# A decode block on one core: w_down's rows and the gate/up columns dealt anew over the partitions, part of them loaded by GpSimd

## The chip, the cores and the metric

One core of one Trainium2 chip. The metric is the device time of one launch in microseconds, the median of the runs shown; lower is better. The kernel before takes 1370.03 us (median of 3 runs, 1370.01 to 1370.21).

## The reference

One token of a decode step. Two branches read the same layer-normed row and are added to the input: attention with a cached K and V of 16384 positions in 32 heads, and a gated feed-forward layer.

```python
D, H, Sk, Dh, Df = 576, 32, 16384, 128, 4608

def _A_ref(x, k_cache, v_cache, wq, wo):
    q = (x @ wq).reshape(B, Sq, H, Dh).transpose(0, 2, 1, 3)
    scores = jnp.einsum("bhqd,bhkd->bhqk", q, k_cache) * (Dh ** -0.5)
    p = _softmax(scores, axis=-1)
    o = jnp.einsum("bhqk,bhkd->bhqd", p, v_cache)
    return o.transpose(0, 2, 1, 3).reshape(B, Sq, H * Dh) @ wo

def _B_ref(x, w_gate, w_up, w_down):
    h = _gelu(x @ w_gate) * (x @ w_up)
    return h @ w_down

xn = _layernorm(x)
return x + _A_ref(xn, ...) + _B_ref(xn, ...)
```

Everything is float32. K and V together are 32 x 2 x 8.4 MB; the weights are wq and wo with 9.4 MB each and w_gate, w_up and w_down with 10.6 MB each.

## The kernel before, in words

All large loads go through SP's queue (`load`, L69, the line under which the profile shows them), in the order in which the code writes them: wq, gate and up, then K and V head by head, then w_down and wo. Four places in SBUF take turns: two K buffers (`kslot`), one V buffer (`vslot`), and small tiles. Each load waits until the earlier user of its buffer is done.

**Projections (`project`, L139).** A weight matrix of 576 rows lies with four rows on each of 128 partitions; the last 64 rows (the tail) are split in two halves of columns so that they also fill 128 partitions. The output columns are dealt to four quarters; quarter q is written to output partitions 32q to 32q+31, so four matmuls use four column groups of TensorE. `sizes` says into which three blocks of one PSUM bank each a quarter's columns are cut. For gate and up a quarter has 4608 / 4 = 1152 columns (`FG`), in blocks of 396, 396 and 360.

**Gate and up (`ffn`).** Column f of gate and up must end on the partition that holds row f of w_down. w_down is loaded with 36 consecutive rows on each partition (`WD_T`), so partition p needs columns 36p to 36p+35. After the matmuls each of the 32 partitions of a quarter holds the whole quarter's row. VectorE multiplies it by the mask `same` (L176), which keeps the partition's own columns, and sums over the 32 groups (L179), which leaves `gu`, 128 x 36 for gate and for up. `ffn_act` makes the activation `hT`, 128 x 36, from it.

**Heads.** For each head VectorE multiplies K by q (L215) and sums (L216), a softmax follows, and TensorE multiplies V by the probabilities (L236, `pv`). K tile h+1 and V tile h are loaded meanwhile.

**The end.** With the last V tile on its way, SP issues w_down in two pieces (`WD_PIECES`: 28 rows a partition into the V buffer `ta`, 8 into the K buffer `tb`) and wo in six (`WO_PIECES`: 16 rows into `tb`, then 8, 4, 2, 1 and 1 into the last buffer `te`). `ta` comes free when TensorE has read the V tile of head 30, `tb` when VectorE has used the K tile of head 31, `te` when TensorE has read the V tile of head 31. TensorE then adds row by row into the output (`add_out`, L281): two matmuls of 288 columns a row, or four of 144 for the last 8 rows of wo. VectorE copies the sum, and ACT stores it as four rows.

GpSimd issues no transfer. Its only work is at the start (a memset and the identity matrix). ACT's queue carries three one-row loads of x and the output.

Of the kernel before, what the change touches and what calls it, by code (L numbers as in the profile page):

```python
# [8 lines left out]
F32 = mybir.dt.float32  # L9
AF = mybir.ActivationFunctionType  # L10
ALU = mybir.AluOpType
AX = mybir.AxisListType

P = 128
H, SK, DH = 32, 16384, 128
D, DF = 576, 4608
# [3 lines left out]
DM = P * DJ  # L20
# [3 lines left out]
HD = H * DH  # L24
QG, QB = HD // 4, 512
QS = HD // 2
WD_T = DF // P
FG = DF // 4
FB = (11 * WD_T, 11 * WD_T, 10 * WD_T)
WO_T = HD // P  # L30
WD_PIECES = (28, 8)
WO_PIECES = (16, 8, 4, 2, 1, 1)
WO_A = 16
WO_Q = 8
QUART = D // 4
HG = 4
# [5 lines left out]
def kernel(ctx: ExitStack, tc: tile.TileContext, x, k_cache, v_cache, wq, wo, wg, wu, wd, out):  # L42
    nc = tc.nc
    cpool = ctx.enter_context(tc.tile_pool(name="cpool", bufs=1))
# [12 lines left out]
    wmain = {n: w[:DM].rearrange("(p j) f -> p (j f)", j=DJ) for n, w in (("q", wq), ("g", wg), ("u", wu))}  # L57
    wtail = {n: w[DM:].rearrange("d (s f) -> (d s) f", s=2) for n, w in (("q", wq), ("g", wg), ("u", wu))}
    wov = wo.rearrange("(p t) f -> p (t f)", t=WO_T)
    wdv = wd.rearrange("(p t) f -> p (t f)", t=WD_T)  # L60

    def kslot():
        return kpool.tile([P, R * DH], F32, tag="k", name="kslot")

    def vslot():
        return vpool.tile([P, R * DH], F32, tag="v", name="vslot")

    def load(dst, src):
        nc.sync.dma_start(dst, src)  # L69
        return dst  # L70

    ROW3 = 3 * DF
    wq_t, wg_t, mix = kslot(), kslot(), vslot()
    qt = load(wg_t[:, ROW3 : ROW3 + QS], wtail["q"])
    load(wq_t, wmain["q"])
    row3, tails, at = {}, {}, 0
# [2 lines left out]
        tails[n] = load(mix[:, at + DF : at + DF + DF // 2], wtail[n])  # L79
        at += DF + DF // 2  # L80

    xrow = mix[:1, ROW3 + FG : ROW3 + FG + D]
    nc.scalar.dma_start(xrow, xf)
    x2 = cpool.tile([P, HALF], F32, name="x2")
    nc.gpsimd.memset(x2, 0.0)
# [11 lines left out]
    same = cpool.tile([P, 32], F32, name="same")  # L97
# [15 lines left out]
    xm = xrow[:, :DM].rearrange("o (p j) -> o j p", j=DJ)  # L113
    for j in range(DJ):
        nc.tensor.matmul(px[:, j : j + 1], xm[:, j, :], ones[:1, :1], start=True, stop=True)
    xd = mix[:1, ROW3 + 2 * FG : ROW3 + 2 * FG + 2 * (D - DM)].rearrange("o (d s) -> o d s", s=2)
    nc.vector.tensor_copy(xd, xrow[:, DM:].unsqueeze(2).to_broadcast([1, D - DM, 2]))
    nc.tensor.matmul(px[:, DJ : DJ + 1], xd.rearrange("o d s -> o (d s)"), ones[:1, :1], start=True, stop=True)
    xp = cpool.tile([P, DJ + 1], F32, name="xp")
# [1 line left out]
    xnb = cpool.tile([P, DJ, 32], F32, name="xnb")  # L121
# [3 lines left out]
    xtb = cpool.tile([P, 2, 32], F32, name="xtb")  # L125
    nc.vector.tensor_copy(xtb, xt.unsqueeze(2).to_broadcast([P, 2, 32]))

    def project(steps, group, sizes):
        pg = ps_big.tile([P, 3, 512], F32, tag="pb", name="pg")
        for k, (j, rhs) in enumerate(steps):  # L130
            for b, size in enumerate(sizes):
                for q in range(4):
                    lo = q * group + sum(sizes[:b])
                    if j < DJ:
                        lhs = xnb[:, j, :]
                    else:
                        lhs = xtb[:, q // 2, :]
                        lo -= q // 2 * 2 * group
                    nc.tensor.matmul(pg[32 * q : 32 * q + 32, b, :size], lhs, rhs[:, lo : lo + size],  # L139
                                     start=k == 0, stop=k == len(steps) - 1)  # L140
        return pg

    steps = [(DJ, qt)] + [(j, wq_t[:, j * HD : (j + 1) * HD]) for j in range(DJ)]
    pq = project(steps, QG, (QB, QB))[:, :2, :]
    qrow = cpool.tile([P, QG], F32, name="qrow")
    nc.scalar.activation(qrow.rearrange("p (b f) -> p b f", f=QB), pq, AF.Copy)

# [2 lines left out]
    def q_spread(h):  # L150
        r = 32 * (h // (H // 4))
        lo = h % (H // 4) * DH
        pq = ps_s.tile([P, 512], F32, tag="sm", name="pq")
        nc.tensor.matmul(pq, ones[r : r + 1, :], qrow[r : r + 1, lo : lo + QH * DH], start=True, stop=True)  # L154
        return pq
# [4 lines left out]
        for i in range(QH):  # L160
            Q[h + i] = qs[:, i : i + 1, :]

    gu = cpool.tile([P, 2, WD_T], F32, name="gu")

    def ffn(which):
        n = "gu"[which]
        t = kslot() if which else wg_t
        steps = [(3, row3[n]), (DJ, tails[n])]
        load(t[:, :ROW3], wmain[n][:, :ROW3])
        steps += [(j, t[:, j * DF : (j + 1) * DF]) for j in range(DJ - 1)]  # L170
        pg = project(steps, FG, FB)
        gm = mix[:, ROW3 : ROW3 + FG].rearrange("p (m t) -> p m t", t=WD_T)
        at = 0
        for b, size in enumerate(FB):
            m = size // WD_T
            nc.vector.tensor_mul(gm[:, at : at + m, :], pg[:, b, :size].rearrange("p (m t) -> p m t", t=WD_T),  # L176
                                 same[:, at : at + m].unsqueeze(2).to_broadcast([P, m, WD_T]))
            at += m
        nc.vector.tensor_reduce(gu[:, which, :], gm.rearrange("p m t -> p t m"), axis=AX.X, op=ALU.add)  # L179

    ffn(0)
    ffn(1)

    hT = cpool.tile([P, WD_T], F32, name="hT")

    def ffn_act():
        g, u = gu[:, 0], gu[:, 1]
        t1 = cpool.tile([P, WD_T], F32, name="t1")
        tc.keep_in_program_order(nc.vector.tensor_mul(t1, g, g))
        tc.keep_in_program_order(nc.vector.tensor_scalar(t1, t1, 0.044715, 1.0, op0=ALU.mult, op1=ALU.add))  # L190
        tc.keep_in_program_order(nc.vector.tensor_mul(t1, t1, g))
        th = cpool.tile([P, WD_T], F32, name="th")
        nc.scalar.activation(th, t1, AF.Tanh, scale=0.7978845608028654)
        t2 = cpool.tile([P, WD_T], F32, name="t2")
        tc.keep_in_program_order(nc.vector.scalar_tensor_tensor(t2, th, 1.0, g, op0=ALU.add, op1=ALU.mult))
        tc.keep_in_program_order(nc.vector.scalar_tensor_tensor(hT, t2, 0.5, u, op0=ALU.mult, op1=ALU.mult))

# [51 lines left out]
    for h in range(H + 1):  # L249
        if h < H:  # L250
            KT[h], n = kslot(), R if h else SUB
            for i in range(0, R, n):
                load(KT[h][:, i * DH : (i + n) * DH], kv[h][:, i * DH : (i + n) * DH])
        if h > 0:
            VT[h - 1] = load(vslot() if h < H else kslot(), vv[h - 1])
        more = (h + 1) % QH == 0 and h + 1 < H
        pq = q_spread(h + 1) if more else None
        if h < H:
            for i in range(0, R, n):
                qk(h, i, n)  # L260
            KT.pop(h)
        if h == 0:
            ffn_act()
        if h > 0:
            pv(h - 1)
            if h % HG == 0:
                out_heads(h - HG)
        if more:
            q_take(h + 1, pq)
        if h < H:  # L270
            softmax(h)
# [6 lines left out]
    def add_out(groups, lhs, w, last=False):  # L278
        n = D // len(groups)
        for i, g in enumerate(groups):  # L280
            nc.tensor.matmul(g, lhs, w[:, i * n : (i + 1) * n], start=id(g) not in seen, stop=last)  # L281
            seen.add(id(g))

    half = [[pairs[i][32 * (2 * i + j) : 32 * (2 * i + j) + 1, :HALF] for j in range(2)] for i in range(2)]
    quart = [acc4[32 * g : 32 * g + 1, :] for g in range(4)]

    def load_rows(t, at, src, lo, n):
        load(t[:, at * D : (at + n) * D], src[:, lo * D : (lo + n) * D])
        return [t[:, (at + j) * D : (at + j + 1) * D] for j in range(n)]

    ta, tb, te = vslot(), kslot(), kslot()
    a, b = WD_PIECES
    wd_rows = load_rows(ta, 0, wdv, 0, a) + load_rows(tb, 0, wdv, a, b)
    wo_rows, lo = [], 0
    for n in WO_PIECES:
        wo_rows += load_rows(tb, b + lo, wov, lo, n) if lo < WO_A else load_rows(te, lo - WO_A, wov, lo, n)
        lo += n
# [13 lines left out]

    for j, w in enumerate(wd_rows):
        add_out(half[j % 2], hT[:, j : j + 1], w)

    for j, w in enumerate(wo_rows):
        if j < WO_T - WO_Q:
# [2 lines left out]
        if j == WO_T - 4:  # L319
            nc.vector.tensor_add(x2[:64], x2[:64], PO[0][64:, :HALF])  # L320
            nc.vector.tensor_add(x2[:64], x2[:64], acc[:64, :HALF])
            for i, g in enumerate(quart):
                r, lo = 32 * (i // 2), i % 2 * QUART
# [34 lines left out]
```

## Time and profile before

| what | value |
|---|---|
| median of 3 runs | 1370.03 us |
| the profiled execution | 1370.16 us |
| its span | 1368.3 us |
| bytes moved | 588.00 MB, mean 430 GB/s |
| VectorE busy | 1135.8 us (83%) |
| TensorE busy | 406.0 us (30%) |
| chain that ended last, by engine | DMA 51%, DVE 46%, PE 2% |

The span runs from the first to the last instruction; the time of the execution is 1.9 us longer. In the rows, a line such as L281 names the line of the kernel, `a<-b,c` the tile written and those read, `x56` a count. In the windows, DMA is the mean busy share of the 16 DMA engines in that stretch: 0.5 means that on average eight of them are at work. The chain is followed back from the last instruction, each piece with its start and its length.

### The profile page before, as it was taken

To read this page: it belongs to the slowest core of one execution; us is meant where nothing else is said; L and a number is where in the kernel's file an instruction comes from. 1 tells how busy PE (TensorE), PEld (TensorE's weight loads), DVE (VectorE), ACT (ScalarE), POOL (GpSimd) and SP (SyncE) were. 2 spreads that over 40 slices of the span, in tenths; PEclk is the share of its full clock that TensorE was granted. 3 is DMA by queue.
4 is the path that set the end of the run, shared out by engine and by line. 5 is a ranking of instruction groups with operands and counts; after the bars stand their busy time and mean duration, and the time that the engine had idled before them with its cause. 6 is when DMAs were issued, how large, how long until landed. Compare 5 with 4: busy or idle time off the path is not lost.

```text
span 1368.3 us, 6377 instructions
## 1 busy us (share of the span) xinstructions
PE 406.0 (30%) x2870; PEld 118.1 (9%) x2870; DVE 1135.8 (83%) x169; ACT 36.5 (3%) x126; POOL 1.0 (0%) x7
## 2 busy tenths in 40 slices
PE   4321233322311232323212332322213333221156
PEld 1110000100000000100000000100001000000012
DVE  1069999899888888898888888998888888988840
ACT  0000000000000000000000000000000000000000
POOL 0000000000000000000000000000000000000000
PEclk8775565565556556565566566565556555665577
DMA  9999999999999999999999999999999999999997
GB/s 404 440 425 450 430 429 430 430 435 432 437 435 429 431 430 439 432 432 435 431 436 433 433 431 430 435 432 439 435 430 430 431 432 437 438 435 428 429 428 336
DMA packets 11704, 588.00 MB, mean 430 GB/s; under 512 B 1303, under 2 KB 1309, under 8 KB 1694
## 3 DMA queue, kind: packets, MB, share of 16 engines
q1 hardware_dynamic: 11664, 587.60, 99.4%
q8 instruction: 22, 0.36, 0.1%
q14 instruction: 4, 0.03, 0.0%
q10 hardware_dynamic: 14, 0.01, 0.0%
HBM read 587.60 MB, written 0.00 MB: 429 GB/s over the span
## 4 chain that ended last, share of the span: by engine, by line
DMA 51%; DVE 46%; PE 2%; issue 0%; SPq 0%; ACT 0%; DVEq 0%
DMA kslot<-in_A_k_cache_dram 41%; DVE s L216 23%; DVE kslot L215 23%; DMA kslot<-in_A_v_cache_dram 3%; DMA kslot<-in_B_w_up_dram 3%; DMA kslot<-in_A_wo_dram 3%; DMA kslot<-in_A_wq_dram 2%; PE pg L139 1%; PE po L236 1%; DVE gu L179 0%; SPq L69 0%; PE pt L222 0%; DVE vslot L176 0%; DVE pm L220 0%; DVE nm L224 0%
## 5 line engine op out<-in xcount | busy, mean ns | idle before, releaser
L215 DVE TENSOR_TENSOR kslot<-kslot,qs 128x16384 f32<-128x16384 f32 (+1 forms) x33 | 551.3, 16705 | 88.4 <-DMA kslot<-in_A_k_cache_dram 86.9
L216 DVE TENSOR_REDUCE s<-kslot 128x128 f32<-128x16384 f32 (+1 forms) x33 | 551.2, 16703 | 3.3
L236 PE MATMUL po<-vslot,pe 128*16 128x512 f32 x1984 | 286.1, 741 | 645.0 <-DMA vslot<-in_A_v_cache_dram 645.0
L236 PEld LDWEIGHTS po<-vslot,pe 128*16 128x16 f32 x1984 | 67.3, 113 | 848.2 <-issue 848.2
L222 PE MATMUL pt<-ident,pm 128*1 128x128 f32 x32 | 11.9, 372 | 236.0 <-DVE pm L220 236.0
L176 DVE TENSOR_TENSOR vslot<-pg,same 128x396 f32<-128x396 f32 (+1 forms) x6 | 3.0, 552 | 69.1 <-PE pg L139 69.1
L139 PE MATMUL pg<-kslot,xnb 128*32 128x396 f32 (+2 forms) x208 | 23.6, 615 | 33.6 <-DMA kslot<-in_B_w_gate_dram 18.9
L228 ACT ACTIVATE nb<-pb 128x1 f32<-128x1 f32 x32 | 5.5, 171 | 812.4 <-PE pb L226 812.4
L320 DVE TENSOR_TENSOR x<-x,po 64x288 f32<-64x288 f32 x1 | 0.5, 457 | 30.8 <-PE po L281 30.8
L222 PEld LDWEIGHTS pt<-ident,pm 128*1 128x1 f32 x32 | 2.5, 79 | 259.4 <-DVE pm L220 218.5
L226 PE MATMUL pb<-nm,ones 1*128 1x1 f32 x64 | 18.1, 350 | 13.2 <-DVE nm L224 13.2
L224 DVE TENSOR_REDUCE nm<-pt 1x1 f32<-1x128 f32 x32 | 8.9, 278 | 14.9 <-PE pt L222 14.9
L226 PEld LDWEIGHTS pb<-nm,ones 1*128 1x128 f32 x64 | 15.8, 305 | 22.2 <-DVE nm L224 11.3
L154 PE MATMUL pq<-qrow,ones 1*128 1x512 f32 x16 | 15.6, 1073 | 0.0
L229 ACT ACTIVATE pe<-s,nb 128x128 f32<-128x128 f32 x32 | 12.8, 401 | 1.0
L302 DVE RECIPROCAL rl<-pl 128x32 f32<-128x32 f32 x1 | 0.4, 358 | 14.9 <-PE pl L300 14.9
L281 PE MATMUL acc<-kslot,oT 128*1 128x144 f32 (+1 forms) x112 | 10.5, 376 | 6.7 <-DMA kslot<-in_A_wo_dram 6.7
L139 PEld LDWEIGHTS pg<-kslot,xnb 128*32 128x32 f32 x208 | 7.1, 126 | 51.0 <-DMA kslot<-in_B_w_gate_dram 19.7
L241 ACT ACTIVATE o<-po 128x512 f32<-128x512 f32 x8 | 4.8, 597 | 222.0 <-PE po L236 222.0
L236 PE MATMUL po<-kslot,pe 128*16 128x512 f32 x64 | 9.6, 769 | 2.6 <-DMA kslot<-in_A_v_cache_dram 2.6
L281 PE MATMUL acc<-vslot,hT 128*1 128x288 f32 x56 | 8.6, 473 | 5.6 <-DMA vslot<-in_B_w_down_dram 5.6
L245 PE MATMUL pc<-same,o 128*128 128x4 f32 x64 | 8.4, 255 | 5.7 <-ACT o L241 5.7
(74 smaller groups left out, 109.9 us busy)
## 6 DMA issues: line engine op xcount, KB each, us to landing
kslot<-in_A_k_cache_dram SPq DMA_DIRECT2D x2, 4096.0 KB
vslot<-in_B_w_down_dram SPq DMA_DIRECT2D x1, 8064.0 KB
kslot<-in_B_w_gate_dram SPq DMA_DIRECT2D x1, 6912.0 KB, 54.0
kslot<-in_B_w_up_dram SPq DMA_DIRECT2D x1, 6912.0 KB
kslot<-in_A_wo_dram SPq DMA_DIRECT2D x1, 4608.0 KB, 39.2
vslot<-in_B_w_gate_dram SPq DMA_DIRECT2D x1, 2304.0 KB, 28.9
vslot<-in_B_w_up_dram SPq DMA_DIRECT2D x1, 2304.0 KB, 37.6
kslot<-in_B_w_down_dram SPq DMA_DIRECT2D x1, 2304.0 KB, 28.7
```

Source lines behind the costliest of these rows:

```text
L139: nc.tensor.matmul(pg[32 * q : 32 * q + 32, b, :size], lhs, rhs[:, lo : lo + size], start=k == 0, stop=k == len(steps) - 1)
L154: nc.tensor.matmul(pq, ones[r : r + 1, :], qrow[r : r + 1, lo : lo + QH * DH], start=True, stop=True)
L215: tc.keep_in_program_order(nc.vector.tensor_mul(blk, blk, Q[h].to_broadcast([P, n, DH])))
L216: nc.vector.tensor_reduce(S[h][:, i : i + n], blk, axis=AX.X, op=ALU.add)
L222: nc.tensor.transpose(pt[:1, :P], pm, ident)
L224: tc.keep_in_program_order(nc.vector.tensor_reduce(nm, pt[:1, :P], axis=AX.X, op=ALU.max, negate=True))
L226: nc.tensor.matmul(pb[:, :1], ones[:1, :], nm, start=True, stop=True)
L228: nc.scalar.activation(nb, pb[:, :1], AF.Copy, scale=SCALE)
L229: nc.scalar.activation(pe4, S.pop(h).rearrange("p (k s) -> p k s", s=4), AF.Exp, bias=nb, scale=SCALE, accum_out=lsum[:, h : h + 1])
L236: nc.tensor.matmul(PO[h // HG % 2][q : q + PW, :], pe[:, lo : lo + PW], vt[:, k * 512 : (k + 1) * 512], start=i == 0 and k < 4, stop=i == ...
L245: nc.tensor.matmul(pc[:, :HG], o4[:, j * DH : (j + 1) * DH], pick[:, j, :], start=j == 0, stop=j == 3)
L281: nc.tensor.matmul(g, lhs, w[:, i * n : (i + 1) * n], start=id(g) not in seen, stop=last)
```

## The change

w_down's rows are dealt unevenly. The first 128 x 33 = 4224 rows are loaded by SP with 33 rows on every partition (pieces of 16 and 17 for 28 and 8). The other 384 rows go to partitions 96 to 127, 12 on each, with four transfers from GpSimd's queue; transfer r takes partitions 96 + r, 100 + r, ..., 124 + r, eight rows of 12 x 2304 B. Before each of them goes a tiny GpSimd transfer of eight rows of 16 B into a part of the buffer that nobody reads.

The columns of gate and up follow: quarters of 32 x 33 = 1056 columns in blocks of 495, 495 and 66, and the last quarter has another 384 in its third block. Where a quarter's block crosses the middle of the tail's columns, its matmul is cut in two. A second, smaller product with the mask and a second sum fill columns 33 to 44 of `gu` on partitions 96 to 127; for the other partitions they stay zero. wo's first piece of 16 becomes 11 and 5, since `tb` now holds 17 rows of w_down. The row of x and a helper row move to another place of the same tile.

```diff
-WD_T = DF // P
-FG = DF // 4
-FB = (11 * WD_T, 11 * WD_T, 10 * WD_T)
+WD_T = 33
+WD_X = 12
+XP = 96
+DX = P * WD_T
+FT = WD_T + WD_X
+FG = 32 * WD_T
+FB = (15, 15, 2)
+FX = 32 * WD_X
 WO_T = HD // P
-WD_PIECES = (28, 8)
-WO_PIECES = (16, 8, 4, 2, 1, 1)
-WO_A = 16
+WD_PIECES = (16, 17)
+WO_PIECES = (11, 5, 8, 4, 2, 1, 1)
+WO_A = 11
...
-    wdv = wd.rearrange("(p t) f -> p (t f)", t=WD_T)
+    wdv = wd[:DX].rearrange("(p t) f -> p (t f)", t=WD_T)
+    wdx = wd[DX:].rearrange("(p t) f -> p (t f)", t=WD_X)
...
-    def project(steps, group, sizes):
+    def project(steps, total, bases, sizes):
         pg = ps_big.tile([P, 3, 512], F32, tag="pb", name="pg")
+        h = total // 2
         for k, (j, rhs) in enumerate(steps):
-            for b, size in enumerate(sizes):
+            for b in range(len(sizes[0])):
                 for q in range(4):
-                    lo = q * group + sum(sizes[:b])
+                    lo = bases[q] + sum(sizes[q][:b])
+                    hi = lo + sizes[q][b]
                     if j < DJ:
-                        lhs = xnb[:, j, :]
+                        parts = [(xnb[:, j, :], lo, hi, 0)]
                     else:
-                        lhs = xtb[:, q // 2, :]
-                        lo -= q // 2 * 2 * group
-                    nc.tensor.matmul(pg[32 * q : 32 * q + 32, b, :size], lhs, rhs[:, lo : lo + size],
-                                     start=k == 0, stop=k == len(steps) - 1)
+                        parts = [(xtb[:, i, :], max(lo, i * h), min(hi, i * h + h), i * h) for i in range(2)]
+                    for lhs, a, e, o in parts:
+                        if a < e:
+                            nc.tensor.matmul(pg[32 * q : 32 * q + 32, b, a - lo : e - lo], lhs, rhs[:, a - o : e - o],
+                                             start=k == 0, stop=k == len(steps) - 1)
...
-    gu = cpool.tile([P, 2, WD_T], F32, name="gu")
+    gu = cpool.tile([P, 2, FT], F32, name="gu")
+    nc.vector.memset(gu, 0.0)
+    fcols = [tuple(m * WD_T for m in FB)] * 3 + [tuple(m * WD_T + FX * (b == 2) for b, m in enumerate(FB))]
...
+        gx = mix[XP:, ROW3 + FG : ROW3 + FG + FX].rearrange("p (m t) -> p m t", t=WD_X)
+        nc.vector.tensor_mul(gx, pg[XP:, 2, FB[2] * WD_T : FB[2] * WD_T + FX].rearrange("p (m t) -> p m t", t=WD_X),
+                             same[XP:, :].unsqueeze(2).to_broadcast([32, 32, WD_X]))
+        nc.vector.tensor_reduce(gu[XP:, which, WD_T:], gx.rearrange("p m t -> p t m"), axis=AX.X, op=ALU.add)
...
-    wd_rows = load_rows(ta, 0, wdv, 0, a) + load_rows(tb, 0, wdv, a, b)
+    wd_rows = load_rows(ta, 0, wdv, 0, a)
+    junk = ta[0:32:4, (a + WD_X) * D : (a + WD_X) * D + 16]
+    for r in range(4):
+        tc.keep_in_program_order(nc.gpsimd.dma_start(junk[:, r * 4 : r * 4 + 4], wdx[r::4, :4]))
+        tc.keep_in_program_order(nc.gpsimd.dma_start(ta[XP + r : P : 4, a * D : (a + WD_X) * D], wdx[r::4, :]))
+    wd_rows += load_rows(tb, 0, wdv, a, b)
+    wd_x = [ta[XP:, (a + j) * D : (a + j + 1) * D] for j in range(WD_X)]
...
     for j, w in enumerate(wd_rows):
         add_out(half[j % 2], hT[:, j : j + 1], w)
+    for j, w in enumerate(wd_x):
+        add_out(half[j % 2], hT[XP:, WD_T + j : WD_T + j + 1], w)
```

More of the change, by code (lines that the diff above doesn't have):

```diff
@@ L80 @@
         at += DF + DF // 2
-    xrow = mix[:1, ROW3 + FG : ROW3 + FG + D]
+    XAT = ROW3 + FG + FX
+    xrow = mix[:1, XAT : XAT + D]
     nc.scalar.dma_start(xrow, xf)
@@ L115 @@
         nc.tensor.matmul(px[:, j : j + 1], xm[:, j, :], ones[:1, :1], start=True, stop=True)
-    xd = mix[:1, ROW3 + 2 * FG : ROW3 + 2 * FG + 2 * (D - DM)].rearrange("o (d s) -> o d s", s=2)
+    xd = mix[:1, XAT + D : XAT + D + 2 * (D - DM)].rearrange("o (d s) -> o d s", s=2)
     nc.vector.tensor_copy(xd, xrow[:, DM:].unsqueeze(2).to_broadcast([1, D - DM, 2]))
@@ L126 @@
     nc.vector.tensor_copy(xtb, xt.unsqueeze(2).to_broadcast([P, 2, 32]))
-    def project(steps, group, sizes):
+    def project(steps, total, bases, sizes):
         pg = ps_big.tile([P, 3, 512], F32, tag="pb", name="pg")
+        h = total // 2
         for k, (j, rhs) in enumerate(steps):
-            for b, size in enumerate(sizes):
+            for b in range(len(sizes[0])):
                 for q in range(4):
-                    lo = q * group + sum(sizes[:b])
+                    lo = bases[q] + sum(sizes[q][:b])
+                    hi = lo + sizes[q][b]
                     if j < DJ:
-                        lhs = xnb[:, j, :]
+                        parts = [(xnb[:, j, :], lo, hi, 0)]
                     else:
-                        lhs = xtb[:, q // 2, :]
-                        lo -= q // 2 * 2 * group
-                    nc.tensor.matmul(pg[32 * q : 32 * q + 32, b, :size], lhs, rhs[:, lo : lo + size],
-                                     start=k == 0, stop=k == len(steps) - 1)
+                        parts = [(xtb[:, i, :], max(lo, i * h), min(hi, i * h + h), i * h) for i in range(2)]
[3 more added lines that the diff above has]
+                                             start=k == 0, stop=k == len(steps) - 1)
         return pg
     steps = [(DJ, qt)] + [(j, wq_t[:, j * HD : (j + 1) * HD]) for j in range(DJ)]
-    pq = project(steps, QG, (QB, QB))[:, :2, :]
+    pq = project(steps, HD, [q * QG for q in range(4)], [(QB, QB)] * 4)[:, :2, :]
     qrow = cpool.tile([P, QG], F32, name="qrow")
@@ L170, in ffn @@
         steps += [(j, t[:, j * DF : (j + 1) * DF]) for j in range(DJ - 1)]
-        pg = project(steps, FG, FB)
+        pg = project(steps, DF, [q * FG for q in range(4)], fcols)
         gm = mix[:, ROW3 : ROW3 + FG].rearrange("p (m t) -> p m t", t=WD_T)
         at = 0
-        for b, size in enumerate(FB):
-            m = size // WD_T
-            nc.vector.tensor_mul(gm[:, at : at + m, :], pg[:, b, :size].rearrange("p (m t) -> p m t", t=WD_T),
+        for b, m in enumerate(FB):
+            nc.vector.tensor_mul(gm[:, at : at + m, :], pg[:, b, : m * WD_T].rearrange("p (m t) -> p m t", t=WD_T),
                                  same[:, at : at + m].unsqueeze(2).to_broadcast([P, m, WD_T]))
             at += m
-        nc.vector.tensor_reduce(gu[:, which, :], gm.rearrange("p m t -> p t m"), axis=AX.X, op=ALU.add)
+        nc.vector.tensor_reduce(gu[:, which, :WD_T], gm.rearrange("p m t -> p t m"), axis=AX.X, op=ALU.add)
+        gx = mix[XP:, ROW3 + FG : ROW3 + FG + FX].rearrange("p (m t) -> p m t", t=WD_X)
+        nc.vector.tensor_mul(gx, pg[XP:, 2, FB[2] * WD_T : FB[2] * WD_T + FX].rearrange("p (m t) -> p m t", t=WD_X),
+                             same[XP:, :].unsqueeze(2).to_broadcast([32, 32, WD_X]))
+        nc.vector.tensor_reduce(gu[XP:, which, WD_T:], gx.rearrange("p m t -> p t m"), axis=AX.X, op=ALU.add)
     ffn(0)
     ffn(1)
-    hT = cpool.tile([P, WD_T], F32, name="hT")
+    hT = cpool.tile([P, FT], F32, name="hT")
     def ffn_act():
         g, u = gu[:, 0], gu[:, 1]
-        t1 = cpool.tile([P, WD_T], F32, name="t1")
+        t1 = cpool.tile([P, FT], F32, name="t1")
         tc.keep_in_program_order(nc.vector.tensor_mul(t1, g, g))
@@ L191, in ffn_act @@
         tc.keep_in_program_order(nc.vector.tensor_mul(t1, t1, g))
-        th = cpool.tile([P, WD_T], F32, name="th")
+        th = cpool.tile([P, FT], F32, name="th")
         nc.scalar.activation(th, t1, AF.Tanh, scale=0.7978845608028654)
-        t2 = cpool.tile([P, WD_T], F32, name="t2")
+        t2 = cpool.tile([P, FT], F32, name="t2")
         tc.keep_in_program_order(nc.vector.scalar_tensor_tensor(t2, th, 1.0, g, op0=ALU.add, op1=ALU.mult))
```

## The prediction, made before the change was run

> **What bounds the kernel now.** I read the transfer rows of the page first, then the chain that ended last, then windows of the last microseconds.
>
> ```profile
> span 1368.3 us, 6377 instructions
> ...
> DMA  9999999999999999999999999999999999999997
> ...
> q1 hardware_dynamic: 11664, 587.60, 99.4%
> q8 instruction: 22, 0.36, 0.1%
> ...
> q10 hardware_dynamic: 14, 0.01, 0.0%
> ```
>
> The 16 DMA engines are busy from one end to the other, so only fewer bytes, less idle time in the last slice, or less cost for each packet can shorten the kernel. The change keeps the bytes. How they lie on engines can be counted: SP issues 81 transfers, and 11664 / 81 = 144 packets = 16 engines x 9, which is eight rows of one of 128 partitions plus a completion. ACT's 14 packets are three one-row loads of x (one row, one completion each, 6) and the four-row output (4 + 4). So a transfer with few rows runs on as many engines as it has rows.
>
> ```profile
> 1275.26 42.84 DMA kslot<-in_A_v_cache_dram
> 1318.10 0.14 issue
> 1318.24 9.66 PE po L236 x64
> ...
> 1329.71 35.08 DMA kslot<-in_A_wo_dram
> 1364.78 0.04 issue
> 1364.83 0.47 PE acc L281 x8
> 1365.30 0.02 issue
> 1365.32 0.31 DVE kslot L328
> ```
>
> The end of the chain: the last piece of wo lands at 1364.78, and 3.5 us of fixed work follow (PE, DVE, the output). The change touches none of these, so the end follows the last landing one for one. Windows up to there (length, busy per engine kind, clock, DMA share, GB/s):
>
> ```profile
> 265.00:1308.00 1043.00, 289.11 (x1869) 79.91 (x1869) 939.82 (x109) 26.17 (x99) 0.00 (x0) 0.61 1.00 433
> ...
> 1358.00:1359.60 1.60, 1.60 (x32) 0.67 (x28) 0.00 (x0) 0.00 (x0) 0.00 (x0) 1.00 0.95 375
> 1359.60:1360.70 1.10, 1.10 (x24) 0.38 (x16) 0.00 (x0) 0.00 (x0) 0.00 (x0) 1.00 0.60 237
> 1360.70:1361.80 1.10, 0.91 (x16) 0.19 (x8) 0.12 (x1) 0.00 (x0) 0.00 (x0) 1.00 0.52 205
> 1361.80:1362.90 1.10, 0.88 (x32) 0.76 (x32) 0.79 (x2) 0.00 (x0) 0.00 (x0) 1.00 0.46 180
> 1362.90:1364.20 1.30, 1.30 (x40) 0.52 (x32) 0.00 (x0) 0.00 (x0) 0.00 (x0) 1.00 0.34 128
> 1364.20:1364.80 0.60, 0.32 (x8) 0.00 (x0) 0.00 (x0) 0.00 (x0) 0.00 (x0) 1.00 0.02 8
> ```
>
> The share falls to one half (0.60, 0.52) and stays there for two windows: about eight engines are done by 1360 to 1361.8, the other eight work on to about 1364.4, though all sixteen got the same bytes. The row of the instruction queue is the likely reason: 22 fetches of 16 KB; 0.1% of 16 x 1368.3 us is 21.9 us, 1.0 us for one. On eight engines these are nearly three each. If the work were dealt so that all ended together, the busy time after 1359.6 (0.60 x 1.1 + 0.52 x 1.1 + 0.46 x 1.1 + 0.34 x 1.3 + 0.01 = 2.2 us) would end at 1361.8: **at most 2.9 us to gain**.
>
> **The change, part by part.**
>
> *Three rows fewer by SP.* 433 GB/s over 16 engines is 27.1 GB/s each. Every engine is spared 3 rows x 8 partitions x 2304 B = 55.3 KB, **-2.04 us on all sixteen**.
>
> *Four large GpSimd transfers* of eight rows of 27.6 KB each. By the count above each runs on eight engines, one row on each; four on the same eight give 110.6 KB, **+4.09 us on those eight**, net +2.05 us there and -2.04 us on the others. What decides is whether the eight are the early or the late ones.
>
> *What a visit of another queue costs an engine* the trace shows only for fetches: 1.0 us for 16.4 KB, where 27.1 GB/s would give 0.61, so 0.39 us more; with the row's rounding (0.05 to 0.15%) 0.5 to 1.5 us, so at most 0.9 more. The GpSimd queue shows no packet here; from below the extra is nothing (ACT's 14 packets hold 0.0%), from above 4 x 0.9 = 3.6 us for four visits. I take 0.8, half of 4 x 0.39, since such a row is larger than a fetch and goes to the same memory as SP's. The four tiny ones cost the other eight between nothing and the same.
>
> *Which eight?* The page numbers no engine. The tiny ones bring 16 B a row that nobody reads; they do something only if consecutive GpSimd transfers take turns on the engines. If the first turn begins where ACT's one-row loads begin, the tiny ones take the half that holds that engine and the large ones the other half. Followed from packet end to packet start in the trace (no view prints this), the engine of the x loads is never held up by an instruction fetch: it belongs to the early eight. Then the large ones fall on the late half. Against it: nothing in the rows says that GpSimd's turns begin there, or that the late eight are exactly a half in that order. Where they are mixed, a late engine is still among the eight, and the end moves alike. Only if the large ones take exactly the early eight does the change gain.
>
> [...]
>
> *Issue and waits.* POOL must wait until the last but one V tile is read, as SP does for the same buffer (rows of the timeline: start, length, what):
>
> ```profile
> 1308.00 0.33 SPq L69 DMA_DIRECT2D vslot<-in_B_w_down_dram  x1
> 1313.98 0.33 SPq L69 DMA_DIRECT2D kslot<-in_B_w_down_dram  x1
> 1314.35 15.79 SPq L69 DMA_DIRECT2D kslot<-in_A_wo_dram  x6
> ...
> 1346.10 0.41 PE L281 MATMUL acc<-kslot,hT 128*1 128x288 f32 x2
> 1346.34 0.41 PE L281 MATMUL acc<-kslot,hT 128*1 128x288 f32 x2
> ...
> 1353.73 0.65 PE L281 MATMUL acc<-kslot,oT 128*1 128x288 f32 x2 [6.00 <-DMA kslot<-in_A_wo_dram]
> ```
>
> Nothing else is queued on POOL then. An issue takes 0.33 us on SP; eight at one to three times that are done by 1311 to 1316. PE wants these rows after 33 others, past 1340: over 20 us of cover, and without it the delay would add to the end only beyond the 6.00 us that PE sits idle for wo. The twelve new rows less the three old ones are nine x 0.24 us (from 1346.10 to 1346.34) = 2.2 us of PE, inside those 6.00. The last pieces of wo keep their sizes. SP issues nine tail transfers for eight; the five wo pieces behind the last V tile go out near 1328 to 1330 and are wanted when some 30 us of wire before them are done, so 0.4 us more is hidden.
>
> *Gate and up.* A quarter's columns go from 396 + 396 + 360 to 495 + 495 + 66, and 450 for the last quarter (rows of the chain, then of the timeline, then of the costliest groups):
>
> ```profile
> 34.50 41.51 DMA kslot<-in_B_w_up_dram
> ...
> 76.05 6.06 PE pg L139 x72
> ...
> 82.13 1.50 DVE vslot L176 x3
> ...
> 83.65 2.04 DVE gu L179
> ...
> 67.79 14.66 SPq L69 DMA_DIRECT2D kslot<-in_A_k_cache_dram  x3
> ...
> 59.59 8.13 PE L139 MATMUL pg<-kslot,xnb 128*32 128x396 f32 x72 [18.88 <-DMA kslot<-in_B_w_gate_dram]
> ...
> L215 DVE TENSOR_TENSOR kslot<-kslot,qs 128x16384 f32<-128x16384 f32 (+1 forms) x33 | 551.3, 16705 | 88.4 <-DMA kslot<-in_A_k_cache_dram 86.9
> ```
>
> 72 matmuls in 6.06 us while one lasts over 0.4 us: the four quarters run side by side, so the longest one counts, 495 + 495 + 450 = 1440 columns for 1152, a quarter more: 2.0 us on the 8.13 and 1.5 on the 6.06. DVE multiplies and sums 1056 columns plus 384 where it had 1152: (1.50 + 2.04) x 288 / 1152 = 0.9 us. So the first K tile is issued near 69.8 instead of 67.79, while up is on the wire until 76.01: 6 us of cover. DVE starts its first head 2.4 us later and has 88.4 us of idle time for K to absorb it. The added memset, 45 columns for 36 in the activation and the moved row of x cost under 1 us on DVE under the same cover. Terms at the end: zero. If K came late, the end would move by as much.
>
> **Sum.** Late half: -2.04 + 4.09 + 0.8 = **+2.85 us**. The profiled run took 1370.16 us (span 1368.3, 1.9 around it), 0.13 above the median of 1370.03, so 1370.03 + 2.85 = **1372.9**. Bounds of this case: +2.05 (no visit cost) to +5.65, 1372.1 to 1375.7.
>
> **Rivals.**
>
> *Early half* (the gain). The large ones take exactly the early eight: their last, near 1361.8, goes to 1363.85 with no visit cost, the late ones come down to 1362.7; the end gains 0.9 us. With 0.8 of visits it gains 0.1, with 1.6 it loses 0.7. 1369.1 to 1370.7, middle **1369.9**. For it: the rows go to partitions 96 to 127 in steps of four, which fits a design for one half; against it: the x loads' engine, above. Even at its best it takes a third of the 2.9 us.
>
> *Spread* (the change doesn't do what it says). The turns don't come out as meant and the large ones alternate between the halves: each engine gets its 55.3 KB back, -2.04 + 2.05, plus two visits of 0.4: **1370.8**, 1370.0 to 1371.8.
>
> *One engine for each large transfer.* Eight rows of 27.6 KB on one engine are 221 KB, 8.2 us, less 2.04: a late one ends 6.1 us later, **1376.2**. Against it stands the packet count of ACT's four-row output, which used four.
>
> *The GpSimd queue itself costs time at the start or end*, or K0 misses its 6 us of cover: at +3 us and more, **1373 and up**. No row speaks for it; POOL has seven instructions in the whole trace.
>
> **How the numbers follow.** Late half 0.45, early half 0.31, spread 0.12, one engine 0.07, the queue or the cover 0.05. The forecast is the likeliest, 1372.9, and its own range 1372.1 to 1375.7. The range 1368.9 to 1375.3 holds nearly all of the early half and the spread and leaves out the late half's highest visit costs and the single engine. 0.2% of 1370.03 is 2.74 us, about what a measurement can tell from no change: slower by more than that (over 1372.77) are two thirds of the late half (0.31), the single engine (0.07), the queue (0.05) and a little of the rest (0.02), 0.45; faster needs nearly the whole 2.9 us, 0.02; the rest, 0.53, lies within.
>
> **What would show it.** In windows of the last 6 us: in the late-half case the share falls to one half some 4 us before the early engines do now relative to the last landing (a gap near 8 us for 4.5), with the last landing near 1367.6; in the early-half case it stays over 0.8 until about a microsecond before the last landing, near 1364. A queue new to the page with four times eight large packets would show the visits; their time against 1.0 us each gives the visit cost. A POOL issue near 1308, PE idle before wo still above 2 us and the first K issue before 72 would show the zeros right. The forecast is wrong if the last landing is earlier than 1366, or if the time moved before 1308.

## The result, and the profile after

| | before | after |
|---|---|---|
| median | 1370.02 us (6 runs, 1369.89 to 1370.21) | 1377.23 us (6 runs, 1375.38 to 1381.0) |
| the profiled execution | 1370.16 us | 1377.67 us |
| its span | 1368.3 us | 1375.9 us |

The change makes the kernel slower, by 7.2 us: after to before is 1.0057, 95% interval 1.0043 to 1.007. The forecast was 1372.9, its range 1368.9 to 1375.3.

The page of the changed kernel, span, transfer rates in 40 slices and queues (packets, MB, share of the engines' time):

```profile
span 1375.9 us, 6481 instructions
...
GB/s 403 438 444 427 431 436 439 427 436 431 440 427 440 427 441 429 441 425 440 433 433 431 437 438 433 427 433 446 429 427 433 450 425 429 435 444 425 432 321 312
...
q1 hardware_dynamic: 11808, 586.72, 99.1%
q0 software_dynamic: 256, 0.89, 0.3%
q8 instruction: 23, 0.38, 0.1%
```

The bytes are the same (586.72 + 0.89 = 587.61 MB for 587.60), and the engines look as busy as ever, but in the last two slices (34.4 us each) they move 321 and 312 GB/s, where they moved 428 and 336 before. Here a busy engine isn't an engine that moves its bytes at full rate. The windows of the tail place it (length, busy time of the engine kinds, clock, DMA share, GB/s). First three of the kernel before:

```profile
1320.00:1326.00 6.00, 6.00 (x48) 1.49 (x44) 0.00 (x0) 0.00 (x0) 0.00 (x0) 0.71 1.06 454
1326.00:1332.00 6.00, 3.76 (x32) 2.00 (x24) 0.84 (x3) 0.97 (x3) 0.00 (x0) 0.86 0.95 410
1332.00:1338.00 6.00, 0.79 (x8) 0.25 (x12) 0.00 (x0) 0.00 (x0) 0.00 (x0) 0.50 0.91 390
```

Then those of the changed kernel:

```profile
1308.00:1314.00 6.00, 0.95 (x3) 0.57 (x3) 3.29 (x3) 0.67 (x3) 2.12 (x5) 0.53 1.11 350
1314.00:1320.00 6.00, 2.65 (x16) 0.69 (x20) 0.00 (x0) 0.00 (x0) 0.00 (x0) 0.50 0.82 316
1320.00:1326.00 6.00, 6.00 (x52) 1.50 (x48) 0.00 (x0) 0.00 (x0) 0.00 (x0) 0.83 1.00 302
1326.00:1332.00 6.00, 2.59 (x20) 1.69 (x12) 0.84 (x3) 0.97 (x3) 0.00 (x0) 0.73 1.07 305
1332.00:1338.00 6.00, 3.96 (x36) 1.27 (x40) 0.00 (x0) 0.00 (x0) 0.00 (x0) 0.50 1.01 330
1338.00:1344.00 6.00, 2.55 (x36) 0.67 (x24) 0.00 (x0) 0.00 (x0) 0.00 (x0) 0.91 0.95 327
...
1364.00:1368.00 4.00, 1.51 (x16) 0.52 (x20) 0.00 (x0) 0.00 (x0) 0.00 (x0) 0.80 0.75 306
1368.00:1372.00 4.00, 3.91 (x78) 1.64 (x74) 0.90 (x2) 0.00 (x0) 0.00 (x0) 0.78 0.12 50
```

For 36 us, while the large GpSimd rows are under way, the share is between 0.82 and 1.11 and the rate is 302 to 350 GB/s, where the kernel before had 433 in its long stage and 390 to 454 in these windows. The end itself is not lopsided as forecast: the share is still 0.75 from 1364 to 1368. The chain that ended last:

```profile
1327.12 39.32 DMA kslot<-in_A_wo_dram
1366.44 0.04 issue
1366.48 0.64 PE acc L296 x2
...
1371.69 1.14 PE acc L296 x32
1372.83 0.02 issue
1372.85 0.31 DVE kslot L351
```

The last pieces of wo now come close together, and TensorE works through them behind the first, 6.4 us from 1366.48 to 1372.85; before, it had 0.5 us left to do behind the last landing. This isn't a new bound: by the records of the single packets in the traces (no view prints them), the output's first packet starts 2.87 us after the last packet of SP's queue, and 2.54 us before the change. So about 0.3 us of the loss is TensorE's, and the rest lies in the transfers.

One row goes the other way. TensorE's start on the last but one V tile, which waits for that tile's landing, before:

```profile
1298.88 9.06 PE L236 MATMUL po<-vslot,pe 128*16 128x512 f32 x64 [21.94 <-DMA vslot<-in_A_v_cache_dram]
```

and after:

```profile
1295.58 9.97 PE L251 MATMUL po<-vslot,pe 128*16 128x512 f32 x64 [21.90 <-DMA vslot<-in_A_v_cache_dram]
```

The changed kernel is 3.3 us *ahead* where the tail begins, in a stage whose transfers the change doesn't touch. So there are two things to explain: some 10 us lost in the tail, and 3.3 us won ahead of it.

The rows for the steps that the prediction put at zero, SP's first K issue (67.79 before) and the GpSimd issues, each in the timeline of the changed kernel:

```profile
68.18 14.94 SPq L75 DMA_DIRECT2D kslot<-in_A_k_cache_dram  x3
```

```profile
1305.90 0.65 POOL L311 DMA_DIRECT2D vslot<-in_B_w_down_dram  x1 [1304.32 <-PE po L251]
1306.54 0.52 POOL L312 DMA_DIRECT2D vslot<-in_B_w_down_dram  x1
...
1309.60 0.52 POOL L312 DMA_DIRECT2D vslot<-in_B_w_down_dram  x1
```

K is asked for 0.4 us later than before and is covered; the eight issues take 4.2 us and are done at 1310.12.

### The profile page after: what moved, and what is told of

Read it like the earlier page. It is cut to its first block, busy times and chain, and to the rows that moved or that the text cites. A ratio compares the mean times of both kernels' runs of the same rounds, so it can differ in the third digit from the quotient of the medians.

```text
span 1375.9 us, 6481 instructions
## 1 busy us (share of the span) xinstructions
PE 413.3 (30%) x2910; PEld 121.9 (9%) x2910; DVE 1138.3 (83%) x174; ACT 36.6 (3%) x126; POOL 5.2 (0%) x15
## 3 DMA queue, kind: packets, MB, share of 16 engines
q1 hardware_dynamic: 11808, 586.72, 99.1%
HBM read 587.60 MB, written 0.00 MB: 427 GB/s over the span
## 4 chain that ended last, share of the span: by engine, by line
DMA 48%; DVE 46%; PE 4%; another core or an unknown queue 1%; issue 0%; ACT 0%; SPq 0%; DVEq 0%
DMA kslot<-in_A_k_cache_dram 40%; DVE s L231 23%; DVE kslot L230 23%; DMA kslot<-in_A_v_cache_dram 3%; DMA kslot<-in_A_wo_dram 3%; PE pg L149 3%; DMA kslot<-in_A_wq_dram 2%; PE po L251 1%; PE acc L296 0%; DVE gu L190 0%; PE pt L237 0%; DVE vslot L187 0%; DVE pm L235 0%; PE pq L164 0%
## 5 line engine op out<-in xcount | busy, mean ns | idle before, releaser
L187 DVE TENSOR_TENSOR vslot<-pg,same 128x495 f32<-128x495 f32 (+1 forms) x6 | 2.8, 516 | 68.4 <-PE pg L149 68.4
L149 PE MATMUL pg<-kslot,xnb 128*32 128x495 f32 (+3 forms) x208 | 25.3, 590 | 30.0 <-DMA kslot<-in_B_w_gate_dram 18.0
L296 PE MATMUL acc<-vslot,hT 128*1 128x288 f32 (+1 forms) x56 | 9.6, 506 | 3.6 <-DMA vslot<-in_B_w_down_dram 3.6
```

The lines of the kernel that those rows point to most:

```text
L149: nc.tensor.matmul(pg[32 * q : 32 * q + 32, b, a - lo : e - lo], lhs, rhs[:, a - o : e - o], start=k == 0, stop=k == len(steps) - 1)
```

## The experiments

The first four runs set the visits of the GpSimd queue against the large rows alone and against their place. All ratios are to the kernel before.

**Eight tiny transfers alone**, put into the kernel before:

```diff
+    junk = ta[0:32:4, a * D : a * D + 32]
+    for r in range(8):
+        tc.keep_in_program_order(nc.gpsimd.dma_start(junk[:, r * 4 : r * 4 + 4], wdv[r : r + 32 : 4, :4]))
```

> The kernel before with nothing added but eight tiny GpSimd transfers (eight rows of 16 B each) into an unused piece of the V buffer, at the place where the change has its eight. Theory V (each GpSimd transfer, large or tiny, holds up all 16 engines; the change's loss of some 7 us divided by eight is 0.7 to 0.9 us a transfer): 1375 to 1377. Theory L (only the four large ones cost): 1370.0 to 1370.5. Theory P (only which engines get the large rows counts): 1370.0.

1370.2 us (10 runs), ratio 1.0001 (0.9992 to 1.001). Visits of the queue cost nothing that can be measured.

**The change without the tiny transfers:**

```diff
-        tc.keep_in_program_order(nc.gpsimd.dma_start(junk[:, r * 4 : r * 4 + 4], wdx[r::4, :4]))
```

> [...] V: half of the visits, about half of the loss, 1373 to 1374. L: the loss of the large ones stays, 1376 to 1378, less up to 2 us if the large ones now fall on both halves. [...]

1376.21 us (1375.57 to 1377.02), ratio 1.0044 (1.0027 to 1.006).

**Each tiny transfer behind its large one** (the two lines changed about):

> [...] V and L alone: no move, 1377 within the change's own spread of 1375.4 to 1381.0.

1376.53 us (1375.8 to 1377.44), ratio 1.0047 (1.0032 to 1.0062). The intervals of this run, the last one and the change lie over each other: whether tiny transfers are there, and on which side, makes no difference. If consecutive transfers took turns on two halves, it would.

**The large rows by SP**, nothing on GpSimd:

```diff
-        tc.keep_in_program_order(nc.gpsimd.dma_start(ta[XP + r : P : 4, a * D : (a + WD_X) * D], wdx[r::4, :]))
+        load(ta[XP + r : P : 4, a * D : (a + WD_X) * D], wdx[r::4, :])
```

> The change with the four large transfers issued by SP, between its two pieces of w_down, and no tiny ones: same rows, same places, no GpSimd queue. V and L: the loss goes, and only where the rows fall is left: 1369.1 if SP's eight-row transfers run on the early eight engines (the engine of the x loads is one of the early ones), 1372.1 if on the late eight. If the new layout, the longer projection or the twelve rows of 32 partitions cost by themselves: 1374 and more.

1376.84 us (1376.2 to 1377.56), ratio 1.0049 (1.0034 to 1.0064): the whole loss without GpSimd. The expectation had such a time only for a layout that costs by itself; the runs from here on separate the layout from the place. Windows of this run:

```profile
1314.00:1320.00 6.00, 5.04 (x32) 1.28 (x36) 0.00 (x0) 0.00 (x0) 0.00 (x0) 0.63 1.08 464
1320.00:1326.00 6.00, 5.00 (x46) 2.04 (x38) 0.25 (x1) 0.77 (x2) 0.00 (x0) 1.00 1.00 220
1326.00:1332.00 6.00, 1.05 (x12) 0.39 (x16) 0.59 (x3) 0.00 (x0) 0.00 (x0) 0.72 0.99 213
1332.00:1338.00 6.00, 5.56 (x62) 1.82 (x52) 0.00 (x0) 0.20 (x1) 0.00 (x0) 0.71 0.95 308
```

On one queue the large rows stand together, and for 12 us sixteen busy engines (1.00, 0.99) move 220 and 213 GB/s: half of 433. A guess to test: the place of these rows, partitions 96 to 127, costs the time. The next four runs set it against the rows' size and steps and the new columns.

**The large rows in partitions 0 to 31**, everything else as in the last run (gate and up get their extra columns there, as a block of its own):

```diff
-XP = 96
+XP = 0
...
-        load(ta[XP + r : P : 4, a * D : (a + WD_X) * D], wdx[r::4, :])
+        load(ta[XP + r : XP + 32 : 4, a * D : (a + WD_X) * D], wdx[r::4, :])
```

> Eight-row transfers by SP as in the kernel without a GpSimd queue, but the twelve extra rows go to partitions 0 to 31 in place of 96 to 127 (transfer r again takes every fourth one; the extra columns of gate and up go to the first quarter, into a PSUM bank of their own). [...] Theory Z (transfers of eight rows, or rows with steps, are slow wherever they go): 1376 to 1377. Theory N (the new layout of w_down costs by itself): 1376.

1368.62 us (11 runs, 1367.34 to 1369.55), ratio 0.9989 (0.998 to 0.9998): 8.2 us less than the last run, and far from the 1376 to 1377 of Z and the 1376 of N. The same windows:

```profile
1314.00:1320.00 6.00, 4.92 (x36) 1.27 (x40) 0.00 (x0) 0.00 (x0) 0.00 (x0) 0.66 1.08 467
1320.00:1326.00 6.00, 5.01 (x50) 2.10 (x46) 0.36 (x1) 0.77 (x2) 0.00 (x0) 1.00 0.98 422
1326.00:1332.00 6.00, 4.27 (x66) 1.75 (x58) 0.48 (x2) 0.20 (x1) 0.00 (x0) 1.00 1.00 431
1332.00:1338.00 6.00, 0.00 (x0) 0.00 (x0) 0.00 (x0) 0.00 (x0) 0.00 (x0) 0.76 0.97 420
```

Same sizes, same steps, same queue, and no dip. From 1320 to 1338 the difference is (202 + 218 + 112) GB/s x 6 us = 3.19 MB, 7.4 us at 433 GB/s, nearly all of the 8.2. The packet records say the same: the 32 packets of the large rows (27,648 B each) took 2.03 us on average in the last run and 1.025 us in this one.

**The same, but each transfer takes eight neighbouring partitions:**

```diff
-        load(ta[XP + r : XP + 32 : 4, a * D : (a + WD_X) * D], wdx[r::4, :])
+        load(ta[XP + 8 * r : XP + 8 * r + 8, a * D : (a + WD_X) * D], wdx[8 * r : 8 * r + 8, :])
```

> As the one before, but transfer r takes eight neighbouring partitions (8r to 8r+7) in place of every fourth one. [...] Z and N: as the one before, no difference between the two.

1377.0 us (2 runs), ratio 1.0051 (1.0032 to 1.0069). The columns, the bytes and the row on each partition are those of the last run; only which eight partitions go into one transfer differs, and the whole loss is back: 8.4 us, where Z and N had no difference. So it isn't the layout, and low partitions alone don't help: what counts is which eight partitions one transfer writes.

**GpSimd, no tiny transfers, partitions 0 to 31** (the edit of the run with low partitions, applied to the one without tiny transfers):

> The four eight-row transfers to every fourth one of partitions 0 to 31, issued by GpSimd, no tiny ones. [...] Z: 1376.

1368.45 us (10 runs, 1367.46 to 1368.94), ratio 0.9988 (0.9979 to 0.9997): as with SP (1368.62), and not Z's 1376.

**One SP transfer of 32 rows to partitions 96 to 127:**

```diff
+    load(ta[XP:, a * D : (a + WD_X) * D], wdx)
```

> The twelve extra rows of partitions 96 to 127 in one SP transfer of 32 rows (two rows on each of 16 engines). [...] Z: no transfer of eight rows is left, 1370 to 1370.5. N: 1376.

1373.91 us (6 runs, 1373.09 to 1375.03), ratio 1.0029 (1.0018 to 1.004): neither Z's 1370 to 1370.5 nor N's 1376. Its SP queue on the page:

```profile
q1 hardware_dynamic: 11856, 587.60, 99.4%
```

82 transfers of 144 packets leave 48, which fits sixteen engines with two rows and a completion each. At 27.1 GB/s two rows are +2.04 us for the -2.04, no net on any engine by that estimate, and still the run is 5.3 us slower than the one with the rows in partitions 0 to 31, where eight engines carried a net of 2.05. The place is left as the cause: a transfer needn't have few rows to lose by it.

**GpSimd and the tiny transfers, partitions 0 to 31** (the tiny line of the change put back into the run before the last):

> The four large GpSimd transfers go to partitions 0 to 31 as in e7_gp_low, but the four tiny ones stand ahead of them again. [...] If all eight-row transfers run on the same eight engines, the tiny ones change nothing: 1368.5 us as e7, 1368.0 to 1369.0.

1368.53 us (10 runs, 1367.29 to 1368.98), ratio 0.9986 (0.9977 to 0.9995). With or without the tiny ones the time is the same (1368.53 and 1368.45): no turns show.

**SP rows into partitions 32 to 63:**

```diff
-XP = 0
+XP = 32
```

> As e5_sp_low, but the twelve rows go to partitions 32 to 63. [...]

1368.59 us (10 runs, 1368.45 to 1368.94), ratio 0.999 (0.9981 to 0.9999). Partitions 32 to 63 are as good as 0 to 31: SP's rows in steps of four gave 1368.62 us in 0 to 31 and 1368.59 in 32 to 63, 1376.84 in 96 to 127, and 1377.0 on eight neighbours of 0 to 31. Why some places cost and others don't, no run shows.

**Two thirds and four thirds of the shift**, SP, partitions 0 to 31: 34 rows and 8, then 32 rows and 16.

```diff
-WD_T = 33
-WD_X = 12
+WD_T = 34
+WD_X = 8
```

> As e5_sp_low with two thirds of the shift: 34 rows a partition and eight more for partitions 0 to 31. All sixteen engines are spared 2 rows x 8 x 2304 B / 27.1 GB/s = 1.36 us and the early eight get 2.72 us back. If the late half sets the end in e5 as it did before, the end comes 0.68 us later than in e5: 1369.0 to 1369.4 us. If the early half already sets it in e5, the end comes earlier or stays: 1368.2 to 1368.6 us.

1371.6 us (11 runs, 1371.38 to 1372.74), ratio 1.0013 (1.0004 to 1.0022). Both cases of the expectation are missed.

> As e5_sp_low with four thirds of the shift: 32 rows a partition and sixteen more for partitions 0 to 31. If the late half still sets the end in e5, the late engines end 0.68 us earlier and the time is 1367.8 to 1368.2 us, the best of the study; if the early eight, which get 0.68 us more, set it by then, 1368.8 to 1369.6 us.

1369.21 us (11 runs, 1367.66 to 1369.58), ratio 0.9993 (0.9984 to 1.0002): the second case, the engines with the large rows set the end.

The miss leads to the other open point. TensorE's start on the last but one V tile in the run with 34 rows:

```profile
1298.78 8.34 PE L257 MATMUL po<-vslot,pe 128*16 128x512 f32 x64 [21.94 <-DMA vslot<-in_A_v_cache_dram]
```

It runs the long stage at the pace of the kernel before (1298.88), not of the change (1295.58). What these two share, and none of the kernels so far that run at the faster pace, is where the three large buffers start. They lie behind the small tiles, each of which takes a multiple of 32 B in the compiled programs. Before, `gu` takes 288 B and `hT`, `t1`, `th`, `t2` 160 B each; in the change 384 and 192, 224 B more in all. In the compiled programs the first K buffer starts at byte 27,680 before, 32 past a multiple of 256, at 27,904 = 109 x 256 in the change, and at 27,872 with 34 rows, 32 past a multiple of 64 (224 past one of 256). The buffers are 65,536 B each, so all three stand alike. The last four runs test it.

**The kernel before with 224 unused bytes:**

```diff
+    cpool.tile([P, 56], F32, name="pad")
     hT = cpool.tile([P, WD_T], F32, name="hT")
```

> The kernel before with an unused tile of 224 B a partition ahead of hT, so that all three large buffers (K, K, V) start where they start in the change: at a multiple of 256 B, where before they start 32 B past one. Theory A (alignment): the long K and V stage runs at the pace that it had in the change, 434 for 433 GB/s (1 MB more by 1308 us), 2.9 us saved over the whole: 1367.1 us (1366.6 to 1367.6). Theory R (the faster stage comes from something else in the change, its columns or its instructions): 1370.0 us as before.

1366.62 us (9 runs, 1366.43 to 1366.79), ratio 0.9975 (0.9965 to 0.9985). One unused tile wins 3.4 us. The same TensorE row and the chain's end:

```profile
1295.45 9.83 PE L237 MATMUL po<-vslot,pe 128*16 128x512 f32 x64 [21.98 <-DMA vslot<-in_A_v_cache_dram]
```

```profile
1360.50 1.31 PE acc L282 x32
1361.81 0.02 issue
1361.83 0.31 DVE kslot L329
```

1298.88 - 1295.45 = 3.43 us are won by the end of the long stage, 0.26% of it, and the end comes 3.5 us earlier (1361.83 for 1365.32). It is the fastest kernel of the study, ahead of both kernels of the case.

**The kernel before with 32 unused bytes** (`[P, 8]` for `[P, 56]`):

> As e13, with 32 B in place of 224: the buffers start at a multiple of 64 B that is 64 B past a multiple of 256. Theory A with 64 B as the size that counts: 1367.1 us as e13. [...] Theory R: 1370.0 us.

1369.29 us (10 runs, 1369.16 to 1369.43), ratio 0.9994 (0.9985 to 1.0003).

```profile
1297.98 9.81 PE L237 MATMUL po<-vslot,pe 128*16 128x512 f32 x64 [21.93 <-DMA vslot<-in_A_v_cache_dram]
```

A start at 64 past a multiple of 256 wins 0.9 us of the 3.4 by that row (1297.98, 1298.88 before, 1295.45 with 224 unused bytes): a multiple of 64 B isn't enough, and the 1367.1 that it would have given is missed by 2.2. The packet records order the kernels alike: a K or V packet of 65,536 B in the long stage takes 2.4239 us on average before, 2.4230 in this run, and 2.4192 in the run with 224 unused bytes and in the change. Why a start at a multiple of 256 B is faster, and why 64 past is a little better than 32 past, no run shows.

**The change with 32 unused bytes**, which puts its buffers 32 past a multiple of 256 again:

> The change with an unused tile of 32 B a partition, so that its buffers start 32 B past a multiple of 256 B as they do before the change. Theory A: the change loses what its sizes had given it by chance, 1377.2 + 2.9 = 1380.1 us (1379 to 1382), and the stage to 1308 us runs at 433 GB/s. Theory R: 1377.2 us.

1382.5 us (4 runs, 1381.21 to 1383.94), ratio 1.0091 (1.0077 to 1.0105).

```profile
1298.80 8.48 PE L252 MATMUL po<-vslot,pe 128*16 128x512 f32 x64 [21.94 <-DMA vslot<-in_A_v_cache_dram]
```

The head start is gone (1298.80). The time lies a little above the range that was expected, and is 5.3 us worse than the change: 3.2 by the row, and 2 more in the tail, which is within the spread of the change's own runs (1375.38 to 1381.0). With its buffers where they were, the change costs 12.5 us, not 7.2.

**34 rows and 8 with 32 unused bytes**, which makes them multiples of 256:

> e11_sp_p0_34, whose tiles put the buffers 32 B past a multiple of 64 B, with 32 B more, so that they start at the multiple of 256 B of e5 and e12. Theory A: 1371.6 - 2.9 = 1368.7 us (1368.2 to 1369.2), in line with e5 (1368.6) and e12 (1369.2). Theory R: 1371.6 us.

1367.93 us (10 runs, 1366.47 to 1368.25), ratio 0.9982 (0.9973 to 0.9991).

```profile
1295.77 9.47 PE L258 MATMUL po<-vslot,pe 128*16 128x512 f32 x64 [22.00 <-DMA vslot<-in_A_v_cache_dram]
```

3.7 us less than without: the miss of the run with 34 rows was the buffers' start. The time lies 0.3 below what was expected.

## Why the prediction was wrong, step by step

Two kernels on the way from before to after split the 7.2 us. Each of the first three rows is the difference of two medians, so they add up to the whole by themselves; what they show is the sizes. The third also changes the queue, which the last row shows to be free.

| step | between | us | in the prediction |
|---|---|---|---|
| buffers at a multiple of 256 B | before, with 224 unused bytes | -3.4 | nothing |
| twelve rows of eight partitions dealt to eight engines, in partitions 0 to 31 | that one, SP rows to 0 to 31 | +2.0 | +2.05 |
| the rows go to partitions 96 to 127 instead | that one, the change | +8.6 | nothing |
| queue visits and tiny transfers | several pairs | 0 | +0.8 |

**The step that failed** is the four large transfers: "four on the same eight give 110.6 KB, +4.09 us on those eight". It priced a packet by its engine's 27.1 GB/s and didn't ask where it is written. The engines' count and their net load were right (see the shift below); that the rows go to partitions 96 to 127 costs 8.6 us more.

The packet records show where it is lost: while these rows are under way, all sixteen engines are slow, not only those that carry them. In the change there is a time when three packets of large rows are in flight, and the thirteen others in flight all take 1.77 to 1.83 times their usual time (1.367 us for a packet of 36,864 B, the median before). The periods with at least one large packet in flight add up to 20.4 us. The 48 packets of w_down's other rows that lie wholly inside them take 1.72 times their usual time on average (1.37 at least), those of the tail wholly outside 1.004 times. 20.4 x (1 - 1 / 1.72) = 8.5 us, the size of the loss. In the run with the same queue and tiny transfers on partitions 0 to 31, packets inside such periods take 1.00 times. The same sum gives 7.3 us of the 8.2 for the SP rows to 96 to 127 (16.3 us, 1.82) and 6.9 us of the 7.3 between the one transfer of 32 rows (14.0 us, 1.97) and 1366.62. For eight neighbours it gives 4.9 us of 8.4 (13.2 us, 1.60), so something more is lost there. Why these places cost, and why all sixteen engines slow down together, no run shows.

**The step that was missing** is the address. The first part had "less cost for each packet" on its list of what can shorten the kernel, and then put "-2.04" and "+4.09" on top of a long stage taken as unchanged; the longer `gu`, `hT`, `t1`, `th` and `t2` were costed as instructions alone, and they moved the large buffers. The prediction's own test said it: the forecast is wrong "if the time moved before 1308", and it did, by 3.3 us the other way. Buffers off a multiple of 256 B cost 3.4 us before, 3.7 with 34 rows and 5.3 in the change; the change's own runs spread over 5.6 us, so whether it is dearer there isn't shown.

**The sum -2.04 + 4.09 held.** With all buffers at multiples of 256 B and the rows in partitions 0 to 31, the time grows with the shift by the net that was worked out:

| shift | rows' net by the prediction's rates | measured, less 1366.62 |
|---|---|---|
| 34 and 8 | +1.36 us | +1.3 (1367.93) |
| 33 and 12 | +2.05 us | +2.0 (1368.62) |
| 32 and 16 | +2.73 us | +2.6 (1369.21) |

So at least one engine that ends late is among the eight, as the sentence on mixed halves had it, and none of the three splits gained. **The early half** (0.31) was therefore wrong in fact, and it was wrong in reading the steps of four into 96 to 127 as a point for it: the steps of four are right (1368.62 us in 0 to 31, 1377.0 on neighbours), the partitions aren't (1376.84).

**The argument for which eight** was wrong, and its result (+2.05 us net) held by luck. It rested on GpSimd's transfers taking turns. No run bears turns out: no tiny ones, tiny ones ahead or behind, SP instead, all within 1376.2 to 1377.2 at partitions 96 to 127 and 1368.4 to 1368.7 at 0 to 31. And on partitions 0 to 31 every one of the 32 large packets takes 1.025 us, with the tiny transfers and without them.

**Visit cost, 0.8 us:** nothing. Eight tiny visits gave 1370.2 for 1370.04, and GpSimd's large rows 1368.45 where SP's gave 1368.62. The sign that the prediction named for it, the time of the large packets, would have misled: they took 1.73 us in the change, by the place and not by the queue.

**The zeros held:** K's first issue came at 68.18, ahead of the 69.8 allowed for; GpSimd's issues ended at 1310.12, ahead of 1311 to 1316. TensorE's longest wait for wo in the tail was 4.34 us after 6.00, above the 2 that the prediction named. The wire was the bound throughout, as the first part said: the DMA row of the changed kernel's page reads 9 in 39 of 40 slices.

**One engine for each large transfer** (0.07) gave 1376.2, the nearest number, by a mechanism that the run in partitions 0 to 31 excludes: the same four transfers by SP took 8.2 us less there.

## What to carry to other kernels

Price a transfer by the partitions that it writes as well as by its engines: in this kernel eight-row transfers cost no more than the load on their engines in steps of four within partitions 0 to 31 or 32 to 63 (1368.45 to 1368.62 us), and slowed the other transfers in steps of four within 96 to 127 or on eight neighbours (1376.21 to 1377.23). The same 885 KB cost 7.3 to 8.6 us by their place, over the 13.2 to 20.4 us that they were under way. Try a start at a multiple of 256 B for large buffers that are loaded by DMA: 224 unused bytes won 3.4 us here (1366.62 for 1370.04), and against that kernel every dealing of rows lost 1.3 us or more. And when two versions differ in the sizes of small tiles, compare where the large buffers start before explaining a difference in a stage that wasn't touched.

## What the runs showed of the hardware that was not expected

- Sixteen engines that read as fully busy (1.00 and 0.99 in the run with SP's rows) moved 213 to 220 GB/s, half the usual 433, while rows dealt over eight engines went to partitions 96 to 127: the busy share doesn't show it, the GB/s column does.
- The slowdown isn't limited to the engines that carry such rows or to eight others: with three of their packets in flight in the change, the other thirteen took 1.77 to 1.83 times as long.
- Buffers that start 32 B past a multiple of 256 B cost 0.26% of the whole load stage here (1298.88 for 1295.45 us), on rows of 64 KiB.
- Eight-row transfers from GpSimd and from SP gave the same time in either place (1376.21 and 1376.84; 1368.45 and 1368.62).
